# One core, float32 layers by split matmuls: the second weight product of the first layer as seven block products, with fourteen weight blocks rounded early into DRAM

## The chip, the cores and the metric

The kernel runs on one core of a Trainium2 chip. The time is device microseconds of one execution, taken as the median of three runs. Engines are named as in the profile: PE (matmuls), PEld (PE's weight loads), DVE, ACT and POOL (vector, scalar and general engines), SP (the queue that issues most DMAs).

## What is computed

A gated linear attention over `B, H, S, D = 2, 8, 768, 64`, then two feed-forward layers over its 1536 tokens of width 512:

```
state = gamma * state + k_t v_t^T ;  attn_t = scale * q_t state
x  = attn                       # (1536, 512)
h  = (x @ w_a) * (x @ w_b)      # (1536, 1536)
y  = h @ w_out                  # (1536, 512)
h2 = y @ w_in ; g = max(0.01 * h2, h2)     # (1536, 2048)
out = g @ w_out2                # (1536, 512)
```

The weights arrive as 64-bit floats, whose bits the kernel reads as pairs of 32-bit words and rounds to float32 itself.

## The kernel before

**Tiles.** All is held transposed: features on 128 partitions, tokens along the row, in three token tiles (t = 0, 1, 2) of 512. A weight block is 128 by 512. There are 12 blocks each of `a`, `b` and `wo` (the first layer, f = 0 to 11) and 16 each of `wi` and `wq` (the second, f = 0 to 15).

**Split matmuls.** A float32 operand is split in two (`split`, line 178): ACT casts it to the high part, DVE subtracts to get the low part. `mm3` (line 185) then issues three matmuls: high by high, high by low, low by high.

**Rounding a weight block.** SP loads 512 KB of raw bits into one of four buffers. `begin_weights` (line 213) has ACT take the magnitude (L220) and DVE the low word (L221); `round_steps` (line 225) adds four DVE instructions: sign (L235), scale and clip (L237), shift and or (L239), and the add of the low word (L243). Blocks are rounded in the order of the list `order`, and the raw buffer is loaded anew after it.

**First layer.** For each f, `ab_step` (line 444) runs 12 matmuls into bank `pa` (x by a) and 12 into `pb` (x by b) for one token tile; ACT copies `pa` out (L439), DVE multiplies the copy by `pb` (L441) and so makes h. `want` splits the next f's weights between the steps, and `ahead` rounds further blocks.

**y.** 36 steps of 12 matmuls follow (`y_mm`, line 463): each takes the split h of one token tile and one f, and adds to four banks over all f. Its side work is the split of h (L181, L182), of `wo`, and more rounding: 26 of the 32 blocks of the second layer are rounded before that layer begins.

**Second layer.** For each f (0 to 15, here called a block), three `h2_step`s make h2 for the three token tiles (12 matmuls each, one bank each; ACT scales it, L590, DVE takes the maximum, L591), and then one product of `Seven` is run. That class computes `g @ w_out2` as a 2 by 2 block product with 7 products in place of 8. The tokens are cut in two halves (tile 0 with half of tile 1, and half of tile 1 with tile 2), the inner index f in two halves, the columns of the weight in two. `prep` (line 113) makes the form of a product for one f: three ACT casts and three DVE subtractions (one of them 512 wide, two 256), and queues the sums of blocks that later products need; `product` (line 143) runs its matmuls: six of 512 columns and six of 256, into three banks. p1 and p7 run between the h2 steps, the other five by themselves after them. PSUM has eight banks; with p1 and p7 both open, two are left for the h2 steps. The last four `wi` blocks (f = 12 to 15) are rounded only when `want` asks for them, after the first h2 step of the block ahead (line 640).

## Time and profile before

| | us |
|---|---|
| median of 3 runs | 602.09 (602.02 to 602.2) |
| the profiled execution | 602.61 |
| its span, first to last instruction | 600.8 |
| PE busy in the span | 588.9 (98%) |
| DVE busy | 438.9 (73%) |
| ACT busy | 243.4 (41%) |
| POOL busy | 16.7 (3%) |

PE's busy time is modelled and overlaps from one matmul to the next, so the stages are measured from start to start: attention to 50.05 us, the first layer's `pa` and `pb` to 246.79, y to 344.71, then the second layer, whose last matmul starts at 596.69. The DMA queues move 52.26 MB at a mean of 87 GB/s.

### The profile page before, as it was taken

To read this page: it belongs to the slowest core of one execution; us is meant where nothing else is said; L and a number is where in the kernel's file an instruction comes from. 1 tells how busy PE (TensorE), PEld (TensorE's weight loads), DVE (VectorE), ACT (ScalarE), POOL (GpSimd) and SP (SyncE) were. 2 spreads that over 40 slices of the span, in tenths; PEclk is the share of its full clock that TensorE was granted. 3 is DMA by queue.
4 is the path that set the end of the run, shared out by engine and by line. 5 is a ranking of instruction groups with operands and counts; after the bars stand their busy time and mean duration, and the time that the engine had idled before them with its cause. 6 is when DMAs were issued, how large, how long until landed. Compare 5 with 4: busy or idle time off the path is not lost.

```text
span 600.8 us, 8357 instructions
## 1 busy us (share of the span) xinstructions
PE 588.9 (98%) x3175; PEld 492.1 (82%) x3175; DVE 438.9 (73%) x880; ACT 243.4 (41%) x499; POOL 16.7 (3%) x20
## 2 busy tenths in 40 slices
PE   6999999999999999999999999999999899999997
PEld 4888788888888888888888888888888777888886
DVE  3894667867777777996979575454666877969992
ACT  3763232223332324544343333333333336878710
POOL 3430000000000000000000000000000000000000
PEclk9999999999999999999999999999999999999999
DMA  8991223323423332321324220000000000010111
GB/s 300 385 355 37 71 105 141 124 91 136 141 105 117 130 123 91 138 78 64 141 78 166 72 71 0 1 0 1 1 1 0 2 0 2 1 53 2 53 53 53
DMA packets 19912, 52.26 MB, mean 87 GB/s; under 512 B 2336, under 2 KB 4000, under 8 KB 19872
## 3 DMA queue, kind: packets, MB, share of 16 engines
q1 hardware_dynamic: 19584, 51.45, 24.1%
q8 instruction: 25, 0.41, 0.3%
q10 hardware_dynamic: 288, 0.27, 0.2%
q14 instruction: 15, 0.12, 0.1%
HBM read 48.57 MB, written 3.15 MB: 86 GB/s over the span
## 4 chain that ended last, share of the span: by engine, by line
PE 94%; DVE 3%; ACT 1%; DMA 1%; issue 1%; POOL 0%; SPq 0%; DVEq 0%; POOLq 0%; ACTq 0%
PE h L187 7%; PE h L188 7%; PE h L189 7%; PE blk L188 6%; PE blk L187 6%; PE blk L189 6%; PE y L189 5%; PE y L187 5%; PE y L188 5%; PE pa L187 5%; PE pa L188 5%; PE pa L189 5%; PE pb L187 5%; PE pb L189 5%; PE pb L188 5%; PE sc L340 2%
## 5 line engine op out<-in xcount | busy, mean ns | idle before, releaser
L188 PE MATMUL blk<-form,form 128*128 128x512 f32 (+1 forms) x224 | 75.7, 338 | 0.0
L187 PE MATMUL blk<-form,form 128*128 128x512 f32 (+1 forms) x224 | 75.5, 337 | 0.0
L189 PE MATMUL blk<-form,form 128*128 128x512 f32 (+1 forms) x224 | 75.2, 336 | 0.0
L591 DVE TENSOR_TENSOR g<-g,h 128x512 f32<-128x512 f32 x48 | 32.6, 685 | 49.3 <-ACT g L590 49.3
L439 ACT COPY p<-pa 128x512 f32<-128x512 f32 x36 | 21.0, 587 | 106.9 <-PE pa L189 105.2
L590 ACT ACTIVATE g<-h 128x512 f32<-128x512 f32 x48 | 28.2, 596 | 86.4 <-PE h L189 86.4
L441 DVE TENSOR_TENSOR h<-p,pb 128x512 f32<-128x512 f32 x36 | 24.7, 686 | 47.6 <-PE pb L189 46.6
L125 ACT CAST form<-g 128x512 fp32r<-128x512 f32 x112 | 53.5, 513 | 12.0 <-DVE g L111 6.4
L126 DVE TENSOR_TENSOR form<-g,form 128x512 fp32r<-128x512 f32 x112 | 57.3, 553 | 0.9
L187 PEld LDWEIGHTS blk<-form,form 128*128 128x128 f32 x224 | 42.5, 190 | 5.4
L188 PEld LDWEIGHTS blk<-form,form 128*128 128x128 f32 x224 | 42.5, 190 | 5.0
L189 PEld LDWEIGHTS blk<-form,form 128*128 128x128 f32 x224 | 42.3, 189 | 4.7
L111 DVE TENSOR_TENSOR g<-g,g 128x512 f32<-128x512 f32 (+1 forms) x56 | 30.7, 573 | 0.3
L126 DVE TENSOR_TENSOR form<-wq,form 128x256 fp32r<-128x256 f32 x56 | 23.5, 420 | 9.2 <-ACT form L125 9.2
L125 ACT CAST form<-wq 128x256 fp32r<-128x256 f32 x56 | 22.7, 404 | 9.6 <-DVE wq L120 7.9
L346 DVE SCALAR_TENSOR_TENSOR P<-sc,small,causal 128x512 f32<-128x512 f32 x24 | 16.8, 742 | 7.4 <-PE sc L340 7.4
L322 POOL TENSOR_TENSOR qs<-q,cst 128x512 f32<-128x512 f32 x12 | 15.3, 1274 | 22.9 <-DMA q<-in_qT 21.4
L340 PE MATMUL sc<-qs,k 64*128 64x128 f32 x192 | 13.9, 285 | 1.5 <-POOL qs L322 1.5
L340 PEld LDWEIGHTS sc<-qs,k 64*128 64x128 f32 x192 | 11.6, 187 | 3.8 <-POOL qs L322 2.6
L319 ACT ACTIVATE kd<-n,small 128x256 f32<-128x256 f32 x24 | 10.9, 501 | 6.5 <-DMA n<-in_kn 6.4
L398 ACT COPY wk<-cr 64x192 f32<-64x192 f32 (+3 forms) x32 | 10.3, 323 | 6.1 <-DVE cr L381 5.5
L409 PE MATMUL xp<-P,v 128*64 128x128 f32 x192 | 12.6, 274 | 0.0
(3377 smaller groups left out, 1547.6 us busy)
## 6 DMA issues: line engine op xcount, KB each, us to landing
raw_wi<-in_w SPq DMA_DIRECT2D x16, 512.0 KB, 3.2
raw_wq<-in_w SPq DMA_DIRECT2D x16, 512.0 KB, 3.2
raw_a<-in_wab SPq DMA_DIRECT2D x12, 512.0 KB, 3.3
raw_b<-in_wab SPq DMA_DIRECT2D x12, 512.0 KB, 3.2
raw_wo<-in_wo SPq DMA_DIRECT2D x12, 512.0 KB, 3.2
q<-in_qT SPq DMA_DIRECT2D x12, 256.0 KB, 5.4
n<-in_kn SPq DMA_DIRECT2D x12, 256.0 KB, 5.3
v<-in_vn SPq DMA_DIRECT2D x12, 256.0 KB, 5.4
```

The lines of the kernel that those rows point to most:

```text
L111: queue.append(lambda piece=piece: run(*(self.A(*x[1:], j)[piece] for x in (d, x0, x1))))
L125: nc.scalar.copy(h, src)
L126: nc.vector.tensor_sub(l, src, h.bitcast(F32))
L187: nc.tensor.matmul(ps, w[0], x[0], start=first, stop=False, skip_group_check=more)
L188: nc.tensor.matmul(ps, w[0], x[1], start=False, stop=False, skip_group_check=more)
L189: nc.tensor.matmul(ps, w[1], x[0], start=False, stop=last, skip_group_check=more)
L340: nc.tensor.matmul(sc[h][:, c], d["k"][r, c], d["qs"][r, c], start=True, stop=True)
L346: nc.vector.scalar_tensor_tensor(pt.rearrange("p (j t) -> p j t", j=CPT), sc[h].rearrange("p (j t) -> p j t", j=CPT), small[:, n:n + 1], m ...
L439: nc.scalar.copy(a, pa)
L441: nc.vector.tensor_mul(h[t, f], a, pb)
L590: nc.scalar.mul(g[t, f], ps, 0.01)
L591: nc.vector.tensor_max(g[t, f], g[t, f], ps)
```

## The change

1. y is computed by the class `Seven` too, with `half` = 6: 42 products of 12 matmuls in place of 36 steps of 12. One of them runs after each f of the first layer (p1 for f = 1 to 6, p7 for f = 7 to 11), the others by themselves.
2. `Seven.prep` becomes a list of portions with a cost in us (`items`). In the first layer all side work (forms, sums, rounding, splits of weights) stands in a list `queue`, and `ab_step` issues 2.5 us of it after the copy of `pa` and 2.05 us after the multiplication by `pb`, 2.0 us more after each product.
3. `order` puts `wo` f-1 behind `a`, `b` f, and 14 blocks of the second layer (wi0 to wi6, wq0 to wq6) among those of the first (`PARK`). Each of the 14 is written to DRAM by a DMA on POOL's queue as soon as it is rounded, and SP loads it back at the end of y or the start of the second layer (`obtain`, `fetch`).
4. The second layer starts with token tile 2 for two values of f, and `want("wi", f + 1)` comes after the second h2 step of a block (after.py line 806) where it came after the first.

The diff, cut to its core:

```diff
 HALF = FF2 // 2
 QT = DM // 2
 LEAD = 3
+LEAD1 = 4
+PARK = (0, 1, 2, 2, 2, 1, 1, 1, 1, 1, 1, 1)
...
     def prep(self, n):
+        for _, run in self.items(n):
+            run()
+
+    def items(self, n):
...
+        def high():
+            hi, lo, x2, w2 = self.form_new(n)
+            (a5, a2), b2 = A(*a, j), B(*b, j)
+            for h, l, src in ((w2[:, 0:QT], w2[:, QT:], b2), (hi, lo, a5), (x2[:, 0:QT], x2[:, QT:], a2)):
+                nc.scalar.copy(h, src)
+                todo.append((l, src, h.bitcast(F32)))
+            todo.append(((hi, lo), (x2[:, 0:QT], x2[:, QT:]), w2))
+            low()
+
+        def low():
+            nc.vector.tensor_sub(*todo.pop(0))
+
+        def done():
+            low()
+            self.forms[n] = todo[0]
+            self.sums(name, j)
...
         if name == "p7":
-            nc.vector.tensor_sub(B(0, 1, j), B(1, 1, j), B(0, 1, j))
...
+            items.append((0.34, lambda: nc.vector.tensor_sub(B(0, 1, j), B(1, 1, j), B(0, 1, j))))
+        return items + [(0.34, high), (0.61, low), (0.34, done)]
...
+    park = ctx.enter_context(tc.tile_pool(name="park", bufs=1, space=bass.MemoryType.DRAM))
...
-    order = [(k, f) for f in range(FF1) for k in ("a", "b")]
-    order += [("wo", f) for f in range(FF1)]
...
     late_wi = [("wi", f) for f in range(FF2 - 4, FF2)]
-    order += [(k, f) for f in range(FF2) for k in ("wi", "wq") if (k, f) not in late_wi] + late_wi
+    second = [(k, f) for f in range(FF2) for k in ("wi", "wq") if (k, f) not in late_wi]
+    order, parked = [("a", 0), ("b", 0)], set()
+    for f in range(1, FF1 + 1):
+        order += [(k, f) for k in ("a", "b") if f < FF1] + [("wo", f - 1)]
+        for _ in range(PARK[f - 1]):
+            order.append(second.pop(0))
+            parked.add(order[-1])
+    first_layer = len(order)
+    order += second + late_wi
...
+        if key in parked:
+            dram[key] = park.tile([P, TT], F32, tag=f"{key[0]}{key[1]}", name=f"{key[0]}{key[1]}")
+            nc.gpsimd.dma_start(dram[key], rounded.pop(key))
+            slots.done(1)
...
+    queue = []
+
+    def pump(us):
+        while queue and us > 0:
+            cost, run = queue.pop(0)
+            run()
+            us -= cost
...
+    def until(done):
+        while queue and not done():
+            queue.pop(0)[1]()
...
+        def end():
+            next(steps[0], None)
+            at["queued"] -= 1
+            if at["queued"] and order[at["round"]] not in begun and at["round"] < at["load"]:
+                begin_weights()
+
...
+        at["queued"] += 1
+        queue.append((0.05, begin))
+        for cost in (0.34, 0.46, 0.72):
+            queue.append((cost, lambda: next(steps[0], None)))
+        queue.append((0.95, end))
+
...
+    def enqueue_split(key):
+        def high():
+            weights[key] = slots.new(F32R, f"{key[0]}{key[1]}h"), slots.new(F32R, f"{key[0]}{key[1]}l")
+            nc.scalar.copy(weights[key][0], rounded[key])
+
+        def low():
+            nc.vector.tensor_sub(weights[key][1], rounded.pop(key), as32(weights[key][0]))
+            slots.done(1)
+
+        queue.extend([(0.05, high), (0.61, low)])
...
+    def obtain(key):
+
+        until(lambda: key in rounded or key in dram)
+        while key not in rounded and key not in dram:
+            round_weights()
+        if key not in rounded:
+            rounded[key] = slots.new(F32, f"{key[0]}{key[1]}")
+            nc.sync.dma_start(rounded[key], dram.pop(key))
+
+    def fetch(n, reserve):
+        for key in list(dram)[:n]:
+            if slots.room() >= 1 + reserve:
+                obtain(key)
...
     def ab_step(t, f):
         pa, pb = bank(f"pa{t}{f}"), bank(f"pb{t}{f}")
         ab_mm(pa, t, f, 0, range(KC))
+        h[t, f] = slots.new(F32, f"h{t}{f}")
+        nc.scalar.copy(h[t, f], pa)
+        pump(2.5)
         ab_mm(pb, t, f, 1, range(KC))
-        ab_out(pa, pb, t, f)
+        nc.vector.tensor_mul(h[t, f], h[t, f], pb)
...
+        pump(2.05)
...
+    def y_split(i, o, m, src):
+
+        if m < 2:
+            y[2 * i, 2 * o + m] = split(src, f"y{i}{o}{m}")
+            return
+        for k in range(2):
+            key = (1, 2 * o + k)
+            if key not in y:
+                y[key] = slots.new(F32R, f"y{o}{k}h"), slots.new(F32R, f"y{o}{k}l")
+            hi, lo = (part[:, i * QT:(i + 1) * QT] for part in y[key])
+            piece = src[:, k * QT:(k + 1) * QT]
+            nc.scalar.copy(hi, piece)
+            nc.vector.tensor_sub(lo, piece, as32(hi))
+
...
+    def finish(z, u, leave):
+        for m in (2, 0, 1):
+            for n in range(len(z.plan) - 2, len(z.plan)):
+                z.product(n, [m])
+            leave(0, 1, [m], u["p1"], nc.vector.tensor_add, z.acc["p3"])
...
-    first = [(t, f) for f in range(1, FF1) for t in range(NTILE)]
-    for n, (t, f) in enumerate(first):
-        if t:
-            want("ab"[t - 1], f + 1)
-        if f == FF1 - 1:
-            h_split(0, t)
-            want("wo", t)
-        ab_step(t, f)
-        ahead(1.3)
...
-    for i, (t, f) in enumerate(late):
-        if i + 3 < len(late):
-            h_split(*late[i + 3])
-        if t == 0:
-            want("wo", f + 3)
-        if t == NTILE - 1 and f >= FF1 - 4:
-            if f >= FF1 - 2:
-                want("wi", f - FF1 + 2)
-        y_mm(t, f)
-        if f == FF1 - 1:
-            y_out(t)
-        slots.tick()
-        ahead(0.35 if t == 0 else 0.6, 9)
...
+    def form1_new(n):
+        new = tnew if n < FF1 - 1 else slots.new
+        return [make(F32R, f"forma{n}") for make in (new, new, tnew, tnew)]
...
+    z = Seven(nc, FF1 // 2, h, lambda f: once(wos, "wo", f), form1_new, blocks, mm3)
+    enqueue_round()
+    for f in range(1, FF1):
+        queue.extend(z.items(f - 1))
+        if f + 1 < FF1:
+            for k in "ab":
+                enqueue_round()
+                enqueue_split((k, f + 1))
+        enqueue_round()
+        for _ in range(PARK[f]):
+            enqueue_round()
+        for t in range(NTILE):
+            ab_step(t, f)
+            if t == 0 and f == FF1 - 1:
+                keep(z, u1, "p1")
+            if t == 1 and f == FF1 - 1:
+                for n in range(FF1 - 1, FF1 + LEAD1 - 2):
+                    queue.extend(z.items(n))
+        until(lambda: f - 1 in z.forms)
+        z.product(f - 1)
+        pump(2.0)
+        queue.extend(z.soon)
+        z.soon.clear()
+        slots.tick()
+    pump(1000)
+    for n in range(FF1 + LEAD1 - 2, FF1 + LEAD1 - 1):
+        z.prep(n)
...
+    H1 = FF1 // 2
+    for n in range(FF1 - 1, len(z.plan) - 2):
+        z.prep(n + LEAD1)
+        if n >= 3 * H1:
+            z.catch_up(2)
+        z.product(n)
+        slots.done(2)
+        slots.tick()
+        name, j = z.plan[n]
...
+        if n in (5 * H1, 6 * H1 - 2):
+            want("wi", int(n != 5 * H1))
+        if j == H1 - 1:
+            combine(z, u1, name, y_leave)
+        if n >= 5 * H1:
+            fetch(1, 12)
+        slots.tick()
+    finish(z, u1, y_leave)
+    slots.done(4 + 3 * H1 + 6)
+    slots.tick()
...
     for f in range(FF2):
-        h2_step(0, f)
-        slots.tick()
-        if f + 1 < FF2:
...
-        if f >= HALF:
-            z.prep(f)
...
-        for t in range(1, NTILE):
-            h2_step(t, f)
...
+        steps = [(t, f) for t in range(NTILE)]
+        if f < 2:
+            steps = [[(2, 0), (2, 1), (0, 0), (1, 0)], [(0, 1), (1, 1)]][f]
+        for n, step in enumerate(steps):
+            h2_step(*step)
             slots.tick()
+            if n == 0 and f == FF2 - 1:
+                keep(z, u2, "p1")
+            if n == 0 and f >= HALF:
+                z.prep(f)
+            if n == (f > 0):
+                if f + 1 < FF2:
+                    want("wi", f + 1)
+                else:
+                    z.prep(FF2)
         if f:
             z.product(f - 1)
         if f < HALF:
             z.prep(f)
         z.catch_up()
         slots.tick()
+        fetch(3, 6)
         if f < FF2 - 4:
-            ahead(1.4, 4)
+            ahead(1.5, 4, len(order) - len(late_wi))
```

What is left out: `combine`, `keep` and `leave` become functions of both layers, with the sums that they made before.

### How the instructions stand, before and now

DVE in the first layer, from one multiplication (L441, now L540) to the next. Names end in buffer numbers: `a8` is block f = 8 of w_a, `a8h`, `a8l` its high and low parts, `h17` is h of token tile 1 and f = 7, `pb17` its bank. Before, from tile 0 to tile 1 of f = 8:

```order
L441 TENSOR_TENSOR h08_237_1959<-p08_236_1957,pb08_1932 128x512
L235 TENSOR_SCALAR sign30_1961<-raw_wo6_1824 128x512
L237 TENSOR_SCALAR wo6_235_1927<-wo6_235_1927 128x512
L239 SCALAR_TENSOR_TENSOR wo6_235_1927<-wo6_235_1927,sign30_1961 128x512
L243 ISA wo6_235_1927<-wo6_235_1927,low30_1928 128x1024
L221 TENSOR_SCALAR low31_1969<-raw_wo7_1869 128x512
L182 TENSOR_TENSOR a9l_240_1973<-a9_193_1501,a9h_239_1972 128x512
L441 TENSOR_TENSOR h18_242_2004<-p18_241_2002,pb18_1977 128x512
```

Now, f = 7, up to the multiplication of tile 1; ahead of these twelve, behind the multiplication of tile 0, stand a subtraction of 256 columns and the low word of a8:

```order
L265 TENSOR_SCALAR sign32_2047<-raw_a8_1885 128x512
L267 TENSOR_SCALAR a8_207_2043<-a8_207_2043 128x512
L269 SCALAR_TENSOR_TENSOR a8_207_2043<-a8_207_2043,sign32_2047 128x512
L273 ISA a8_207_2043<-a8_207_2043,low32_2044 128x1024
L251 TENSOR_SCALAR low33_2055<-raw_b8_1916 128x512
L321 TENSOR_TENSOR a8l_211_2075<-a8_207_2043,a8h_210_2074 128x512
L265 TENSOR_SCALAR sign33_2078<-raw_b8_1916 128x512
L267 TENSOR_SCALAR b8_208_2054<-b8_208_2054 128x512
L269 SCALAR_TENSOR_TENSOR b8_208_2054<-b8_208_2054,sign33_2078 128x512
L273 ISA b8_208_2054<-b8_208_2054,low33_2055 128x1024
L251 TENSOR_SCALAR low34_2086<-raw_wo7_1960 128x512
L540 TENSOR_TENSOR h17_209_2072<-h17_209_2072,pb17_2059 128x512
```

Where four rounding steps, one low word and one split stood, there are now a whole rounding and most of the next one, and the parts of a form.

DVE where y's products begin to run by themselves (`forma14` is the form of product 14 of y, `h05` and `wo5` blocks that are summed). Before, at the first steps of y (`hs00l` is the low part of h):

```order
L182 TENSOR_TENSOR hs00l_2347<-h00_128_889,hs00h_2346 128x512
L182 TENSOR_TENSOR wo0l_278_2351<-wo0_211_1695,wo0h_277_2350 128x512
L441 TENSOR_TENSOR h011_280_2382<-p011_279_2380,pb011_2355 128x512
L235 TENSOR_SCALAR sign41_2384<-raw_wq2_2239 128x512
L237 TENSOR_SCALAR wq2_276_2342<-wq2_276_2342 128x512
L239 SCALAR_TENSOR_TENSOR wq2_276_2342<-wq2_276_2342,sign41_2384 128x512
L243 ISA wq2_276_2342<-wq2_276_2342,low41_2343 128x1024
```

Now, between the forms of products 13 and 14, the last eight of twelve sums and then the forms:

```order
L113 TENSOR_TENSOR h14_175_1560<-h14_175_1560,h110_241_2574 128x256
L113 TENSOR_TENSOR h05_184_1682<-h211_257_2795,h05_184_1682 128x512
L113 TENSOR_TENSOR h15_187_1739<-h111_255_2749,h15_187_1739 128x256
L110 TENSOR_TENSOR wo5_190_1752<-wo11_251_2722,wo5_190_1752 128x256
L113 TENSOR_TENSOR h25_193_1791<-h25_193_1791,h211_257_2795 128x512
L113 TENSOR_TENSOR h15_187_1739<-h15_187_1739,h111_255_2749 128x256
L110 TENSOR_TENSOR wo6_201_1918<-wo0_137_970,wo6_201_1918 128x256
L110 TENSOR_TENSOR wo7_212_2085<-wo1_143_1059,wo7_212_2085 128x256
L138 TENSOR_TENSOR forma14_2868<-wo8_223_2270,forma14_2868 128x256
L138 TENSOR_TENSOR forma14_265_2866<-h08_217_2184,forma14_264_2865 128x512
L138 TENSOR_TENSOR forma14_2867<-h18_219_2236,forma14_2867 128x256
L138 TENSOR_TENSOR forma15_2878<-wo9_234_2439,forma15_2878 128x256
```

The splits of h and of `wo` are gone; sums and forms of the block products stand in their place.

DVE in the second layer, block 12, around the rounding of wi13 (`g12`, `g112` are maxima of token tiles 0, 2 and 1, `form12` the form of product 12). Before, behind the maximum of tile 0:

```order
L221 TENSOR_SCALAR low65_4329<-raw_wi13_3305 128x512
L235 TENSOR_SCALAR sign65_4332<-raw_wi13_3305 128x512
L237 TENSOR_SCALAR wi13_416_4328<-wi13_416_4328 128x512
L239 SCALAR_TENSOR_TENSOR wi13_416_4328<-wi13_416_4328,sign65_4332 128x512
L243 ISA wi13_416_4328<-wi13_416_4328,low65_4329 128x1024
L182 TENSOR_TENSOR wi13l_418_4338<-wi13_416_4328,wi13h_417_4337 128x512
L120 TENSOR_TENSOR wq4_294_2524<-wq12_341_3241,wq4_294_2524 128x256
L126 TENSOR_TENSOR form12_4345<-wq4_294_2524,form12_4345 128x256
L126 TENSOR_TENSOR form12_4343<-g04_375_3685,form12_4342 128x512
L126 TENSOR_TENSOR form12_4344<-g14_378_3705,form12_4344 128x256
L591 TENSOR_TENSOR g112_4365<-g112_4365,h2112_4352 128x512
L591 TENSOR_TENSOR g12_4325<-g12_4325,h2212_4368 128x512
```

Now, behind the same maximum:

```order
L146 TENSOR_TENSOR wq4_362_3600<-wq12_417_4300,wq4_362_3600 128x256
L138 TENSOR_TENSOR form12_4773<-wq4_362_3600,form12_4773 128x256
L138 TENSOR_TENSOR form12_4771<-g04_399_4042,form12_4770 128x512
L138 TENSOR_TENSOR form12_4772<-g14_400_4058,form12_4772 128x256
L759 TENSOR_TENSOR g112_4793<-g112_4793,h2112_4780 128x512
L251 TENSOR_SCALAR low65_4797<-raw_wi13_4397 128x512
L265 TENSOR_SCALAR sign65_4800<-raw_wi13_4397 128x512
L267 TENSOR_SCALAR wi13_447_4796<-wi13_447_4796 128x512
L269 SCALAR_TENSOR_TENSOR wi13_447_4796<-wi13_447_4796,sign65_4800 128x512
L273 ISA wi13_447_4796<-wi13_447_4796,low65_4797 128x1024
L205 TENSOR_TENSOR wi13l_449_4806<-wi13_447_4796,wi13h_448_4805 128x512
L759 TENSOR_TENSOR g12_4766<-g12_4766,h2212_4809 128x512
```

The rounding and the split moved from ahead of the form and of the second maximum to behind both.

## Rows read from the trace of the kernel before

**Rows 1.** The page's head and its part 1, busy time of each engine
```profile
span 600.8 us, 8357 instructions
PE 588.9 (98%) x3175; PEld 492.1 (82%) x3175; DVE 438.9 (73%) x880; ACT 243.4 (41%) x499; POOL 16.7 (3%) x20
```

**Rows 2.** Busy time (and instructions) of each engine in three stretches, with the granted clock (PEclk)
```profile
core 0: us, PE busy (x) PEld busy (x) DVE busy (x) ACT busy (x) POOL busy (x), PEclk, DMA share, GB/s
246.80:344.70 97.90, 97.90 (x433) 81.07 (x432) 79.66 (x150) 40.70 (x71) 0.00 (x0) 1.00 0.30 103
344.70:508.80 164.10, 161.07 (x746) 134.18 (x745) 106.72 (x211) 59.20 (x122) 0.00 (x0) 1.00 0.02 7
508.80:600.80 92.00, 88.28 (x505) 77.19 (x503) 73.48 (x163) 51.22 (x124) 0.00 (x0) 1.00 0.10 35
```

**Rows 3.** Timeline of PE, first matmul of y and first of the second layer
```profile
246.79 0.39 PE L187 MATMUL y<-hs00h,wo0h 128*128 128x512 f32 x1
...
344.71 0.39 PE L187 MATMUL h<-y00h,wi0h 128*128 128x512 f32 x1
```

**Rows 4.** Timeline of PE, one block product in a stretch without waits
```profile
540.23 0.40 PE L187 MATMUL blk<-form,form 128*128 128x512 f32 x1
540.46 0.40 PE L188 MATMUL blk<-form,form 128*128 128x512 f32 x1
...
541.62 0.28 PE L187 MATMUL blk<-form,form 128*128 128x256 f32 x1
541.73 0.28 PE L188 MATMUL blk<-form,form 128*128 128x256 f32 x1
...
542.33 0.40 PE L187 MATMUL blk<-form,form 128*128 128x512 f32 x1
```

**Rows 5.** Timeline of PE, from the product ahead of block 12 into that block
```profile
465.58 0.28 PE L189 MATMUL blk<-form,form 128*128 128x256 f32 x1
466.61 0.50 PE L187 MATMUL h<-y00h,wi12h 128*128 128x512 f32 x1 [0.76 <-DVE g L591]
```

**Rows 6.** Timeline of DVE, what stands ahead of that PE wait
```profile
461.53 0.69 DVE L243 CUSTOM_DVE_ANT_0 wi<-wi,low 128x1024 uint16<-128x1024 uint16 x1
462.91 0.69 DVE L182 TENSOR_TENSOR wi12l<-wi,wi12h 128x512 fp32r<-128x512 f32 x1 [0.69 <-ACT wi12h L181]
...
464.93 1.03 DVE L126 TENSOR_TENSOR form<-g,form 128x512 fp32r<-128x512 f32 x2
465.88 1.28 DVE L591 TENSOR_TENSOR g<-g,h 128x512 f32<-128x512 f32 x2
```

**Rows 7.** Timeline of DVE, one rounding of a weight block and its split
```profile
72.97 0.69 DVE L441 TENSOR_TENSOR h<-p,pb 128x512 f32<-128x512 f32 x1 [2.12 <-PE pb L189]
73.58 0.42 DVE L221 TENSOR_SCALAR low<-raw_a 128x512 int32<-128x512 uint32 x1
...
74.25 0.42 DVE L237 TENSOR_SCALAR a<-a 128x512 f32<-128x512 f32 x1
74.70 0.69 DVE L239 SCALAR_TENSOR_TENSOR a<-a,sign 128x512 int32<-128x512 int32 x1
75.43 0.69 DVE L243 CUSTOM_DVE_ANT_0 a<-a,low 128x1024 uint16<-128x1024 uint16 x1
76.04 0.42 DVE L221 TENSOR_SCALAR low<-raw_b 128x512 int32<-128x512 uint32 x1
76.81 0.69 DVE L182 TENSOR_TENSOR a2l<-a,a2h 128x512 fp32r<-128x512 f32 x1 [0.35 <-ACT a2h L181]
```

**Rows 8.** A group of ACT by line and shape: xcount, busy us, mean ns, idle before
```profile
L439 ACT COPY p<-pa 128x512 f32<-128x512 f32 x36 | 21.0, 587 | 106.9 <-PE pa L189 105.2 <-PE pb L188 1.7
```

**Rows 9.** Timeline of POOL and of DVE in the attention stage, and POOL's line (min/median/max)
```profile
27.20 1.27 POOL L322 TENSOR_TENSOR qs<-q,cst 128x512 f32<-128x512 f32 x1 [1.47 <-DMA q<-in_qT]
...
27.61 1.15 DVE L235 TENSOR_SCALAR sign<-raw_a 128x512 int32<-128x512 int32 x1
...
L322 POOL TENSOR_TENSOR qs<-q,cst x12: 1264/1273/1286, 6.0 to 39.0; 128x512 f32<-128x512 f32 x12
```

168 lines of the change are left out of this document (77 added, 91 removed).

## The prediction

> **What bounds the kernel now.** I read the page's first part, the stages, and then the gaps between matmuls. PE is busy for 588.9 of 600.8 us [rows 1]. That figure is modelled, so I check it by starts. y runs from 246.79 to 344.71: 97.92 us for its 432 matmuls of 512 columns, 0.2267 us each [rows 3]. A block product in a quiet stretch takes 542.33 - 540.23 = 2.10 us [rows 4]: six matmuls of 512 columns at 0.23 and six of 256 at 0.12, no slower per column than y's. So each of these stretches is PE working without a pause, at a granted clock of 1.00 [rows 2], and only less PE work or fewer PE waits can shorten the kernel. DVE is the next busiest; it has 79.66 us of work in y's 97.90 [rows 2], so it has room, but not much.
>
> The waits that exist: between the last matmul of product 11 and block 12 of the second layer PE starts 1.03 us apart, where 0.12 is normal behind a matmul of 256 columns [rows 4, 5]. The releaser is DVE's maximum. Ahead of it DVE rounded wi12, stood idle 0.69 us for ACT's cast, split, made a form and came to the maxima at 465.88 [rows 6]. With p1 and p7 open there are two banks for h2, and the second is handed back by the second maximum. There are four such waits (blocks 12 to 15), 4 x 0.91 = 3.6 us.
>
> **DVE's prices**, from start to start: a two-input operation of 512 columns 0.61 (72.97 to 73.58), each fast step 0.335 (two from 73.58 to 74.25), then 0.45, 0.73 and 0.61 to the start of the next operation: one rounding is 2.46 us [rows 7]. A pair of 512 and 256 takes 0.95 (464.93 to 465.88), so 256 columns cost 0.34 [rows 6]. A split right behind its rounding, with one low word between, loses 0.35 waiting for ACT [rows 7].
>
> **The change, part by part.**
>
> *PE work.* y becomes 42 products of 2.10 us, 88.2 us against 97.92: **-9.7 us**. This is seven products for eight, so it cannot fail to be saved where PE is not made to wait.
>
> *First layer.* From f = 1 to 11, PE works 3 x 24 x 0.2267 + 2.10 = 18.4 us per f. DVE's heaviest are f = 2 to 4: five roundings 12.3, two splits 1.2, one form (0.34 + 0.61 + 0.34) 1.3, sums 1.3, three multiplications 1.8: 17.9, with the ACT wait 18.3. From f = 8 it is four roundings 9.8, splits 1.2, a p7 form 1.6, sums 2.2, multiplications 1.8: 16.7. So DVE fits, by 0.1 us at worst, with 1.7 in hand later. The order decides the rest: from f = 7 both accumulators are open and two banks remain, so `pb` of one step must be multiplied before `pb` of the next begins, 2.72 us later. The longest row is tile 0 to tile 1 at f = 7: behind the end of `pb` come 0.61 + 0.34 + 0.335, then the listed rows, 2.125 + 0.335 + 0.35 + 0.61 + 2.125 + 0.335, which puts the multiplication at 7.2 and its end at 7.9 us. PE wants the bank at 5.44 + 2.72 = 8.16. It holds with 0.2 us to spare. ACT has a copy of 0.59 [rows 8] in the same window, and one late cast eats the rest, so for the five blocks I take **+0.6** (bounds 0 and 5 x 0.91, the size of the waits that two banks make now [rows 5]).
>
> *Where the products run alone.* DVE comes to this stage without a lead. At f = 11, counted from the end of tile 0's `pb`: multiplication, form, a rounding and three steps of another end at 5.5; a multiplication, two steps and a sum at 7.8. The next forms wait for casts that stand behind ACT's copy of the third `pa` (8.16 + 0.59 = 8.75); nine subtractions and a multiplication end near 13.9, twelve sums (4 x 0.61 + 8 x 0.34) near 19.1. PE wants form 14 at 2 x 5.44 + 4 x 2.10 = 19.3, and its second subtraction ends only at 20.1: **+0.8** (bounds 0 and 2). From there to product 41 DVE has 28 forms, 36.1; 31 more operations of 512 columns, 18.9, and 18 of 256, 6.1; less the 3.7 behind the last product: 57.4. PE has 27 x 2.10 = 56.7. DVE is the slower by 0.7, and the last product wants its form's last part some 0.5 sooner than DVE gives it: **+1.2** (bounds 0, if ACT's and DVE's order leaves slack I do not see, and 5.6, below).
>
> *Stores and loads.* 14 roundings move from y to the first layer, counted above. The 14 stores run on POOL, which is idle from 50 us on, and the 14 loads on SP, whose queue holds nothing that is wanted before them. No row shows a store from POOL. The nearest is POOL's multiplication of 1.27 us, during which a DVE step that takes 0.42 elsewhere took 1.15 [rows 7, 9]. At 0.73 each the 14 would add 10 us to DVE, but each comes at an f's end, behind the last rounding, where the next multiplication is 7.5 us after the one before: taken as nothing. Against it, f = 2 to 4 hold two stores and 0.1 us of room; with five banks free there, a lag of some us costs PE nothing, and f = 5 and 6, with 15.4 us of DVE work, take it back.
>
> *Second layer.* The wait behind the maxima goes, as form and second maximum now stand ahead of the rounding: **-3.6**. Late next is the low part of wi. From the end of the first h2 step: maximum 1.3, form 3.7, second maximum 4.3, rounding 6.8, ACT's cast 7.4, low part 8.1; PE wants it at 2 x 2.72 + 2.10 + 0.45 = 8.0: +0.2 for each of four, **+0.8** (bounds 0 and 3.6, all as before). At its start, block 1 has two steps only, and wi2's low part stands behind a form, sums, a rounding and three maxima: about 8.6 us after the last step of block 0 where PE wants 8.0: **+0.5**. The 18 roundings left here are at most two to a block beside 10.26 us of PE work: no wait. The tail is unchanged.
>
> Sum: -9.7 - 3.6 + 0.6 + 0.8 + 1.2 + 0.8 + 0.5 = -9.4. The profiled execution took 602.61, 0.5 above the median, so 602.1 - 9.4 = **592.7 us**.
>
> **The rivals.**
>
> 1. *No new wait at all.* If ACT and DVE run somewhat closer than I add them, all five plus terms are nothing: 602.1 - 13.3 = 588.8. For it: DVE's work fits everywhere within 1 us. Against: at three places it fits with nothing left.
>
> 2. *DVE becomes the bound where products run alone.* Some sums read what the operation ahead wrote; the dependent scale step takes 0.45 where its neighbours take 0.335 [rows 7]. If each of 28 products costs DVE 0.2 us more than I count, PE waits 5.6 us more: 598.3. For it: 57.4 us of work against 56.7, no lead. Against: the second layer's own products ran alone with the same forms, and PE was busy for 88.28 of 92.00 us there, the tail of 3.9 us behind the last matmul among them [rows 2].
>
> 3. *The stores choke, and the kernel is slower.* In the first layer DVE has some 0.6 us in 18.4 free. POOL and DVE shut each other out in the one row that shows them together [rows 9]; there POOL came first. The Trainium skill says so as a rule (SBUF — State Buffer, "Who interferes with whom"): the port pair that the two share is held by one of them for a whole instruction, and a DMA from GpSimd's queue needs it for its descriptors. The trace agrees with the first half: 0.42 became 1.15 us; no run here shows the second. If 1.27 us of POOL work got only the gaps, a store would take two f, 39 us. Seven stores must be out by the last step of f = 7, when their buffers are reused, some 5.5 f or 101 us after the first; so it decides from 14 us a store. At 20 us each, PE waits 7 x 20 - 101 = 39 us: 632. Against: POOL's twelve multiplications kept 1.26 to 1.29 us beside a busy DVE [rows 9]. By the same skill (DMA: Bandwidth & Descriptors, "Anatomy of one DMA — SWDGE (gpsimd) path") a transfer of 262 KB is an estimated 2.0 + 0.6 = 2.6 us, far below 14.
>
> 4. *Two banks cost what they save.* If every step of f = 7 to 11 were late by 0.7 us, one DVE operation, 15 x 0.7 = 10.5 would go: 602.9, no change.
>
> **How the numbers follow.** The forecast, 590 to 596 us, gets 0.65; rival 1 0.13, rival 2 0.13, rival 3 0.05, rival 4 0.04. The range takes in the forecast, rival 1 and the lower half of rival 2: 588.6 to 597.5, which leaves out under 0.2. A measurement of this kernel can tell some 0.2%, 1.2 us, from no change. Faster by more than that: 0.65 + 0.13 + 0.13 = 0.91; the same 0.04; slower 0.05.
>
> **What would show it.** In the new profile, a y product should take PE 2.10 us wherever it runs; the gap into blocks 12 to 15 should fall from 1.03 to some 0.3 us, then released by the low part of wi. There should be a gap of about 0.8 us at product 14, released by DVE, and gaps of a few tenths after it. POOL's stores should land within 14 us. The forecast is wrong if the steps of f = 7 to 11 show a wait for the multiplication at each `pb`, if the product stage of y is longer than 31 x 2.10 + 3 us, or if anything waits for a store.

## The result and the profile after

| | before | after |
|---|---|---|
| median of 4 runs each, us | 602.06 (601.95 to 602.2) | **594.57** (594.24 to 595.14) |
| ratio | 1 | 0.9872, 95% interval 0.9859 to 0.9885 |
| span of the profiled execution | 600.8 | 593.2 |
| PE busy, share of the span | 588.9 (98%) | 583.0 (98%) |
| DVE busy, share of the span | 438.9 (73%) | 502.6 (85%) |

The kernel is 7.5 us faster; 592.7 was forecast, with 588.6 to 597.5 as the range. The head of the page and its part 1 answer to [rows 1]: PE does less, and DVE carries 64 us more, among it the forms and sums of 42 products.

```profile
span 593.2 us, 8767 instructions
PE 583.0 (98%) x3247; PEld 488.8 (82%) x3247; DVE 502.6 (85%) x1049; ACT 270.1 (46%) x587; POOL 24.6 (4%) x34
```

The first question is in which stage the 7.6 us of span went. The timeline of PE (start and length in us, line, tiles) gives the stage starts and the price of a product. Before, the first matmul of the first layer and the last of the second:

```profile
50.05 0.48 PE L187 MATMUL pa<-x0h,a0h 128*128 128x512 f32 x1
...
596.69 0.39 PE L189 MATMUL blk<-form,form 128*128 128x512 f32 x1
```

Now, the same two, with a product of y and the first matmul of the second layer between them:

```profile
50.31 0.48 PE L210 MATMUL pa<-x0h,a0h 128*128 128x512 f32 x1
...
280.04 0.40 PE L210 MATMUL blk<-forma,forma 128*128 128x512 f32 x1
...
282.14 0.40 PE L210 MATMUL blk<-forma,forma 128*128 128x512 f32 x1
...
337.51 0.39 PE L210 MATMUL h<-y100h,wi0h 128*128 128x512 f32 x1
...
589.16 0.39 PE L212 MATMUL blk<-form,form 128*128 128x512 f32 x1
```

A y product takes 282.14 - 280.04 = 2.10 us, as in [rows 4]. From the first `pa` to the first matmul of the second layer it was 344.71 - 50.05 = 294.66 us before [rows 3] and is 337.51 - 50.31 = 287.20 now: -7.46. From there to the last matmul it was 251.98 and is 251.65: only -0.33. Attention ends 0.26 us later, which says nothing: it ends anywhere from 49.18 to 51.10 in the runs below, whose code for it is the same. So the first layer and y gave what was forecast (-7.1), and the second layer, forecast at -2.3, gave almost nothing.

The busy time of each engine in three stretches (columns as in [rows 2]: PE, PEld, DVE, ACT and POOL with instructions in brackets, then the granted clock) shows where PE pauses. The first stretch ends where the product after f = 11 starts, the second is that product and the 31 after it, the third the second layer up to its own products alone:

```profile
50.31:268.18 217.87, 217.54 (x988) 180.53 (x986) 189.70 (x386) 78.96 (x151) 7.74 (x14) 1.00 0.39 136
268.18:337.51 69.33, 68.42 (x385) 59.02 (x384) 67.28 (x149) 43.27 (x108) 0.00 (x0) 1.00 0.17 54
337.51:501.23 163.72, 162.85 (x746) 133.71 (x745) 134.97 (x271) 67.12 (x135) 0.00 (x0) 1.00 0.13 46
```

PE waits for nothing between 84 and 268 us, from f = 2 to 11: two banks were enough. In the products alone DVE is busy 67.28 of 69.33 us. In the third stretch PE is idle 0.87 us by the model; the starts show more. Here is PE at the step into block 13, to be held against [rows 5]:

```profile
470.68 0.28 PE L212 MATMUL blk<-form,form 128*128 128x256 f32 x1
470.99 0.50 PE L210 MATMUL h<-y000h,wi13h 128*128 128x512 f32 x1
471.32 0.40 PE L211 MATMUL h<-y000l,wi13h 128*128 128x512 f32 x1
471.71 0.50 PE L212 MATMUL h<-y000h,wi13l 128*128 128x512 f32 x1
472.05 0.39 PE L210 MATMUL h<-y001h,wi13h 128*128 128x512 f32 x1
```

The single wait of 0.91 us is gone, and two have come in its place: 0.31 where 0.12 is normal (for wi13's high part), then 0.39 where 0.23 is normal (for its low part). Behind each of the two the next matmul also starts 0.33 to 0.34 us later in place of 0.23. Together 0.57 us, the same at blocks 14 and 15, and 0.51 at block 12: 2.2 us. What stands ahead of it, in the timeline of DVE and ACT (idle time before the instruction and its releaser in brackets):

```profile
465.68 0.42 DVE L138 TENSOR_TENSOR form<-wq,form 128x256 fp32r<-128x256 f32 x1 [0.48 <-ACT form L132]
...
467.14 0.68 DVE L759 TENSOR_TENSOR g<-g,h 128x512 f32<-128x512 f32 x1
467.74 0.42 DVE L251 TENSOR_SCALAR low<-raw_wi 128x512 int32<-128x512 uint32 x1
...
469.59 0.69 DVE L273 CUSTOM_DVE_ANT_0 wi<-wi,low 128x1024 uint16<-128x1024 uint16 x1
470.32 0.62 ACT L204 CAST wi13h<-wi 128x512 fp32r<-128x512 f32 x1 [2.79 <-DVE wi L273]
...
470.97 0.69 DVE L205 TENSOR_TENSOR wi13l<-wi,wi13h 128x512 fp32r<-128x512 f32 x1 [0.69 <-ACT wi13h L204]
```

The order is the one forecast. But DVE idles 0.48 us for the form's cast, and only then comes the second maximum and, behind it, the whole rounding.

Two further waits on a split, at block 2 and at block 9, on PE again:

```profile
356.14 0.40 PE L211 MATMUL h<-y000l,wi2h 128*128 128x512 f32 x1
357.10 0.50 PE L212 MATMUL h<-y000h,wi2l 128*128 128x512 f32 x1 [0.57 <-DVE wi2l L205]
...
428.91 0.40 PE L211 MATMUL h<-y000l,wi9h 128*128 128x512 f32 x1
429.52 0.50 PE L212 MATMUL h<-y000h,wi9l 128*128 128x512 f32 x1 [0.22 <-DVE wi9l L205]
```

At block 2 PE loses 0.85 us (0.96 for 0.23, then 0.34 for 0.23), at block 9 some 0.57. Last, the wait at product 14, where DVE, ACT and PE have to be read together:

```profile
265.66 0.59 ACT L537 COPY h<-pa 128x512 f32<-128x512 f32 x1 [4.23 <-PE pa L212]
...
266.58 0.43 DVE L138 TENSOR_TENSOR forma<-wo,forma 128x256 fp32r<-128x256 f32 x1 [1.29 <-ACT forma L132]
...
276.55 0.39 PE L210 MATMUL blk<-forma,forma 128*128 128x512 f32 x1
277.36 0.50 PE L211 MATMUL blk<-forma,forma 128*128 128x512 f32 x1 [0.41 <-DVE forma L138]
```

PE loses 0.58 + 0.11 us there, and some 1.5 us more at five shorter waits for forms up to 334 us. Ten us earlier DVE stood idle 1.29 us: the casts of product 11's form stand on ACT behind the copy of the third `pa`, and that waits for PE.

POOL's stores, by their line (seven of wi shown, the seven of wq likewise; duration ns, min/median/max, and first and last start; then the time to landing of all 14):

```profile
L279 POOL DMA_DIRECT2D wi<-wi x7: 539/542/712, 89.0 to 254.6; - x7
...
DMA to landing us min/median/max: 2.3/2.4/3.2
```

### The profile page after: what moved, and what is told of

The parts are those of the page before. It is cut to its first block, busy times and chain, and to the rows that moved or that the text cites. A ratio compares the mean times of both kernels' runs of the same rounds, so it can differ in the third digit from the quotient of the medians.

```text
span 593.2 us, 8767 instructions
## 1 busy us (share of the span) xinstructions
PE 583.0 (98%) x3247; PEld 488.8 (82%) x3247; DVE 502.6 (85%) x1049; ACT 270.1 (46%) x587; POOL 24.6 (4%) x34
## 4 chain that ended last, share of the span: by engine, by line
PE 79%; DVE 17%; ACT 2%; issue 1%; ACTq 0%; DVEq 0%
PE blk L211 8%; PE blk L210 8%; PE blk L212 8%; PE h L212 7%; PE h L210 7%; PE h L211 7%; DVE forma L138 6%; PE pa L210 5%; PE pa L211 5%; PE pa L212 5%; PE pb L212 5%; PE pb L210 5%; PE pb L211 5%; DVE h L113 2%; PE sc L431 1%
## 5 line engine op out<-in xcount | busy, mean ns | idle before, releaser
L537 ACT COPY h<-pa 128x512 f32<-128x512 f32 x33 | 19.4, 588 | 101.3 <-PE pa L212 101.3
L211 PE MATMUL blk<-forma,forma 128*128 128x512 f32 (+1 forms) x168 | 57.4, 342 | 0.9 <-DVE forma L138 0.7
L210 PE MATMUL blk<-forma,forma 128*128 128x512 f32 (+1 forms) x168 | 56.6, 337 | 0.0
L212 PE MATMUL blk<-forma,forma 128*128 128x512 f32 (+1 forms) x168 | 56.5, 336 | 0.0
L138 DVE TENSOR_TENSOR forma<-h,forma 128x512 fp32r<-128x512 f32 x84 | 42.9, 549 | 0.5
L132 ACT CAST forma<-h 128x512 fp32r<-128x512 f32 x84 | 38.8, 511 | 0.0
L211 PEld LDWEIGHTS blk<-forma,forma 128*128 128x128 f32 x168 | 31.8, 189 | 6.1 <-DVE forma L138 2.3
L210 PEld LDWEIGHTS blk<-forma,forma 128*128 128x128 f32 x168 | 31.8, 189 | 4.0
L212 PEld LDWEIGHTS blk<-forma,forma 128*128 128x128 f32 x168 | 31.7, 189 | 3.3
```

What stands on the lines that cost most here:

```text
L132: nc.scalar.copy(h, src)
L138: nc.vector.tensor_sub(*todo.pop(0))
L210: nc.tensor.matmul(ps, w[0], x[0], start=first, stop=False, skip_group_check=more)
L211: nc.tensor.matmul(ps, w[0], x[1], start=False, stop=False, skip_group_check=more)
L212: nc.tensor.matmul(ps, w[1], x[0], start=False, stop=last, skip_group_check=more)
L537: nc.scalar.copy(h[t, f], pa)
```

## The experiments

The theory after this reading: the second layer waits for the split of the next wi, by where the split stands, and y's waits come from the order of casts on ACT. The rivals: DVE's whole work is the bound; the stores on POOL slow DVE; two banks are too few. The table gives each run's median, its ratio to the kernel before with its interval, and two lengths from its profile: first layer and y (first `pa` to first h), and second layer (first h to last matmul).

| run | us | ratio | first layer and y | second layer |
|---|---|---|---|---|
| the changed kernel | 594.57 | 0.9872 (0.9859 to 0.9885) | 287.20 | 251.65 |
| e1_want_first | 596.47 | 0.9902 (0.9887 to 0.9916) | 287.20 | 252.83 |
| e2_want_mixed | 594.21 | 0.9865 (0.985 to 0.988) | 287.20 | 251.05 |
| e3_late_early | 592.6 | 0.9838 (0.9822 to 0.9855) | 287.25 | 249.37 |
| e4_park13 | 598.21 | 0.9937 (0.9919 to 0.9956) | 287.18 | 255.71 |
| e9_forms_first | 593.9 | 0.9858 (0.9843 to 0.9873) | 286.65 | 251.59 |
| e5_all | 590.93 | 0.981 (0.9795 to 0.9824) | 286.60 | 248.75 |
| e7_lumps | 601.75 | 0.9991 (0.9981 to 1.0) | 293.74 | 251.59 |
| e10_all_13 | 593.23 | 0.9847 (0.9823 to 0.9871) | 285.72 | 252.16 |
| e6_store_sp | 594.65 | 0.9869 (0.9855 to 0.9882) | 287.24 | 251.58 |
| e8_nopark | 626.49 | 1.0396 (1.0377 to 1.0415) | 297.80 | 272.41 |
| e11_moved_14 | **589.67** | **0.9788** (0.9775 to 0.9801) | 285.71 | 248.19 |
| e12_moved_15 | 589.64 | 0.9787 (0.9773 to 0.9801) | 285.75 | 247.89 |

### Where the split of the next wi stands

e1_want_first puts all splits behind the first h2 step:

```diff
-            if n == (f > 0):
+            if n == 0:
                 if f + 1 < FF2:
                     want("wi", f + 1)
```

> The changed kernel, with every split of the next wi put back behind the first h2 step of its block, late blocks included. Theory (the second layer still waits for the split of the next wi, and the place of the split decides which wait there is): the four late blocks get back the wait for the second maximum, 4 x 1.03 us in place of 4 x 0.57, +1.8; the wait at block 2 (0.85 us) mostly goes, -0.6, the one at block 9 (0.57 us) goes; together +0.7 us, about 595.3. Rival A (the place does nothing; what is late is DVE's whole work in that layer): within 0.3 us of the changed kernel. Rival B (the prediction's prices: the waits of 0.91 us come back and waits of 0.2 go): +2.8 us, 597.4.

Slower by 1.9 us in the median, 1.2 in the second layer's length. The late blocks lost what was expected: 1.03 us at each, from 458.87 on, and the wait at block 2 fell from 0.97 to 0.37 us between starts. What did not come is the gain at block 9: waits of 0.51 us in all turned up in block 10. So the place of the split matters at block 2 and at the late blocks, and not at block 9.

e2_want_mixed keeps the later place for the late blocks alone:

```diff
-            if n == (f > 0):
+            if n == (f >= FF2 - 5):
```

> The changed kernel, with the split of the next wi behind the first h2 step for blocks 2 to 11, and behind the second only for the four late blocks. Theory (the waits at blocks 2 and 9 come from the split standing behind a maximum that it need not stand behind): both go or shrink to 0.3 us, -1.1 us, 593.5, with the late blocks as they were. Rival A (DVE's whole work is late there, after two roundings in a row): the waits turn up at another instruction, within 0.3 us of the changed kernel.

The second layer is 0.60 us shorter, all of it at block 2; the median's -0.36 is within the runs' spread. Block 9's wait moved to block 10's start (0.37 us where 0.12 is normal). The theory holds for block 2 and the rival for block 9: there DVE had two roundings in a row behind it (both done at 424.85 in the changed kernel, just ahead of block 8's form), and is late wherever the split stands.

### The late roundings in two parts

e3_late_early fills DVE's idle time ahead of the form with the rounding's first steps:

```diff
-            if n == 0 and f >= HALF:
+            if n == 0 and FF2 - 5 <= f < FF2 - 1:
+                part = round_steps()
+                items = [run for _, run in z.items(f)]
+                for run in items[:-3] + [lambda: next(part)] * 2 + items[-3:]:
+                    run()
+            elif n == 0 and f >= HALF:
                 z.prep(f)
...
+                if FF2 - 5 <= f < FF2 - 1:
+                    for _ in part:
+                        pass
                 if f + 1 < FF2:
                     want("wi", f + 1)
```

> The changed kernel, with the roundings of the four late wi in two parts: magnitude, low word, sign and scale ahead of the form of p7, shift and add behind the second maximum as before. Theory (the low part of wi ends 0.45 us too late at blocks 12 to 15, and DVE stands idle 0.48 us ahead of the form for ACT's cast): the low part comes 0.55 us earlier, the four waits of 0.57 us go, -2.2 us, 592.4. Rival (DVE's work per block, not its order, is the bound; the form and the second maximum come 0.45 us later and a wait turns up there): between -0.5 and 0.

As the theory said: -2.0 us in the median, -2.28 in the second layer. The timeline of DVE shows three steps of the rounding in the time for which it used to wait, and the split's low part starts at 469.17, 0.71 us ahead of block 13's first matmul:

```profile
464.20 0.42 DVE L251 TENSOR_SCALAR low<-raw_wi 128x512 int32<-128x512 uint32 x1
464.53 0.42 DVE L265 TENSOR_SCALAR sign<-raw_wi 128x512 int32<-128x512 int32 x1
464.87 0.42 DVE L267 TENSOR_SCALAR wi<-wi 128x512 f32<-128x512 f32 x1
465.21 0.42 DVE L138 TENSOR_TENSOR form<-wq,form 128x256 fp32r<-128x256 f32 x1
...
469.17 0.69 DVE L205 TENSOR_TENSOR wi13l<-wi,wi13h 128x512 fp32r<-128x512 f32 x1 [0.69 <-ACT wi13h L204]
```

And PE goes into block 13 without a pause:

```profile
469.76 0.28 PE L212 MATMUL blk<-form,form 128*128 128x256 f32 x1
469.88 0.40 PE L210 MATMUL h<-y000h,wi13h 128*128 128x512 f32 x1
```

### Where y's waits come from

e4_park13 leaves one rounding, at f = 11, to the second layer:

```diff
-PARK = (0, 1, 2, 2, 2, 1, 1, 1, 1, 1, 1, 1)
+PARK = (0, 1, 2, 2, 2, 1, 1, 1, 1, 1, 1, 0)
```

> The changed kernel, with 13 weight blocks rounded into DRAM in place of 14: the rounding of wq6 at the end of the first layer (2.46 us of DVE) is left to the second layer. Theory (DVE's work bounds the products that run alone in y, without a lead): the waits at product 14 and behind it, 2.2 us in all, go, and the second layer takes the rounding beside its 10.26 us of PE per block: -2.0 us, 592.6. Rival A (those waits come from the order of casts and forms): they stay, within 0.4 us of the changed kernel. Rival B (the work is only handed on, and the second layer waits for it): the stage of y is shorter by 2 us and the second layer longer by as much.

The theory missed: 2.46 us less DVE work ahead of y's products, and the stage is as long as before (287.18). DVE only idles longer for the same casts, 2.55 us in place of 1.29:

```profile
267.35 0.42 DVE L138 TENSOR_TENSOR forma<-wo,forma 128x256 fp32r<-128x256 f32 x1 [2.55 <-ACT forma L132]
```

So rival A holds for these casts, and rival B's second half too: the second layer is 4.06 us longer. There DVE rounds two blocks in a row at 442.70 to 447.28 with two banks left, and PE waits for the first maximum of block 10:

```profile
445.45 0.39 PE L212 MATMUL h<-y11h,wi10l 128*128 128x512 f32 x1
448.01 0.50 PE L210 MATMUL h<-y100h,wi10h 128*128 128x512 f32 x1 [2.18 <-DVE g L759]
...
449.65 0.63 PE L210 MATMUL h<-y110h,wi10h 128*128 128x512 f32 x1
450.08 0.63 PE L211 MATMUL h<-y110l,wi10h 128*128 128x512 f32 x1
```

The wait costs 2.3 us, and from 449.65 on matmuls start 0.43 us apart for some three us, at a lower granted clock: 1.6 us more (see the last section). Of the four runs two show that clock in their mean (0.997: 598.47 and 600.14, the profiled one) and two do not (1.000: 597.74 and 597.96), so the median stands between the two.

e9_forms_first issues two forms ahead of the last step of the first layer:

```diff
                 for n in range(FF1 - 1, FF1 + LEAD1 - 2):
                     queue.extend(z.items(n))
+                until(lambda: FF1 in z.forms)
```

> The changed kernel, with the forms of products 11 and 12 issued ahead of the last step of the first layer, so that their casts on ACT stand ahead of the copy of the third pa and no longer behind it. Theory (the waits at product 14 and behind it come from ACT's order: DVE stands idle 1.29 us for these casts at 266.58 and never makes it up): DVE has that much lead, the wait of 0.69 us at product 14 goes and those behind it shrink, -1.2 us, 593.4. Rival A (DVE's work in the stage bounds it, whatever its lead): the later waits grow by what is saved, within 0.3 us of the changed kernel. Rival B (the copy of the third pa is wanted sooner, and the multiplication and PE wait for it): slower by 0.3 to 1 us.

Half of it: -0.7 us in the median, -0.55 in the stage. DVE's idle time for the cast falls to 0.47 us, and the wait at product 14 is gone; the waits behind it stay. That DVE's work is what counts for those is shown by e10_all_13 below: with the forms first and one rounding less, the stage is another 0.9 us shorter.

```profile
265.48 0.43 DVE L138 TENSOR_TENSOR forma<-wo,forma 128x256 fp32r<-128x256 f32 x1 [0.47 <-ACT forma L132]
```

e5_all has the edits of e2_want_mixed, e3_late_early and e9_forms_first together:

> Three edits at once on the changed kernel: the mixed place of the split, the late roundings in two parts, and the forms of products 11 and 12 ahead of the last step of the first layer. Theory (three separate waits): the gains add, -0.4, -2.0 and -1.2 us, 591.0. Rival (what one edit frees is taken by the next wait): 592.0 to 592.6, no better than the late roundings in two parts alone.

The three edits together give -3.6 us, against -0.4, -2.0 and -0.7 alone. In the lengths they add to within 0.05 us: -0.60 in the first layer and y against -0.55 alone, -2.90 in the second layer against -0.60 and -2.28. So these are separate waits, and what one edit frees is not taken by another.

### Portions, stores and DRAM

e7_lumps issues the first layer's side work once a step:

```diff
-        pump(2.5)
+        pass
...
-        pump(2.05)
+        pump(4.55)
```

> The changed kernel, with the first layer's side work issued in one portion of 4.55 us behind each multiplication by pb in place of two of 2.5 and 2.05. Theory (DVE has the work done in time either way; pb's bank is wanted 2.1 us after the multiplication could run, and a portion of 4.55 fits between two of them): 0 to +1.5 us, 595.3. Rival A (the portions are what keeps PE going with two banks): a wait of 0.7 us or more at each step of f = 7 to 11, +10 us or more. Rival B (fewer interleavings save ACT's waits): -0.5 us.

Slower by 7.2 us, nearly all of the change's gain, so rival A is nearer in size; but its place is another. PE waits for the copy of `pa`, not for the multiplication (waits of PE in 84 to 345 us: total, times, longest):

```profile
PE blk L211 <- DVE forma L138: 2.9, 3, 2.3
PE pa L210 <- ACT h L537: 2.5, 4, 1.7
```

The lump's work on ACT stands ahead of the copy: at f = 8 ACT is at the magnitude of `a` until the copy's start at 207.02, and PE starts the next `pa` 0.66 us behind the last `pb` in place of 0.23. At f = 9 and 10 it is the same, at f = 11 it is 2.11 us, as ACT's three copies of p1's banks (L576) stand there too: 3.6 us in all. Most of the rest is lost at product 14, to which DVE comes later still: 2.73 us between starts there in place of 0.81. In two portions the copy stands between them. (The profiled run, 601.37, and one other, 600.70, have a mean granted clock of 1.000; the other eight, 601.3 to 602.6, have 0.997.)

e6_store_sp moves the stores to SP's queue:

```diff
-            nc.gpsimd.dma_start(dram[key], rounded.pop(key))
+            nc.sync.dma_start(dram[key], rounded.pop(key))
```

> The changed kernel, with its 14 stores to DRAM issued on SP's queue in place of POOL's. Theory (the stores cost nothing on POOL: no DVE instruction beside one is stretched): within 0.3 us, 594.6. Rival A (POOL's issuing shuts DVE out for a part of each store): -0.5 to -2 us. Rival B (a store on SP holds up the weight loads behind it): +1 us or more.

No change (594.65 against 594.57, ratio 0.9869 against 0.9872). The stores cost nothing that the time shows on POOL's queue, and on SP's neither.

e8_nopark rounds nothing early:

```diff
-PARK = (0, 1, 2, 2, 2, 1, 1, 1, 1, 1, 1, 1)
+PARK = (0,) * 12
...
-            ahead(1.5, 4, len(order) - len(late_wi))
+            ahead(2.0, 4, len(order) - len(late_wi))
```

> The changed kernel without the early roundings: no block goes through DRAM, and the second layer rounds 28 blocks, up to two after each block. Theory (DVE has 17 us idle from the second layer's start to block 11, and 14 more roundings are 14 x 2.46 = 34 us): PE waits some 17 to 25 us there, the waits in y go (-1.9), 610 to 618, slower than the kernel before. Rival (the second layer has room for the roundings): 593 to 597.

Slower than the kernel before by 24 us and than the changed kernel by 32. The second layer grew by 20.8 us, as expected; that y's waits would go was wrong: y grew by 10.6, since the splits of wi0 and wi1 now bring their roundings into it. Not all of this is waiting: behind some of the pauses the granted clock is 0.50, for 17.1 us in four stretches (from 336.6, 343.4, 370.7 and 486.8), where matmuls start 0.43 us apart. By these starts that is some 6 of the 32 us. The largest wait of PE in the second layer up to 503 us:

```profile
PE h L210 <- ACT wi12h L204: 8.0, 1, 8.0
```

So the change depends on the early roundings through DRAM: without them DVE has no room, at the end of y and in the second layer, for both the roundings and the block products.

### A better version

e10_all_13 is e5_all with 13 blocks and another rate of rounding in the second layer:

```diff
-PARK = (0, 1, 2, 2, 2, 1, 1, 1, 1, 1, 1, 1)
+PARK = (0, 1, 2, 2, 2, 1, 1, 1, 1, 1, 1, 0)
...
-            ahead(1.5, 4, len(order) - len(late_wi))
+            ahead(2.0 if f < 7 else 1.0, 4, len(order) - len(late_wi))
```

> The three edits at once, with 13 blocks rounded into DRAM in place of 14, and the second layer's rounding ahead at two a block up to block 6 and one a block from 7. Theory (the 2.57 us wait of the 13-block run came from two roundings in a row in a late block; early blocks have room for two): y's waits go by another 0.6 us and nothing is given back, 590.4. Rival A (two roundings in every early block are over DVE's room): waits at blocks 1 to 7, slower than the three edits alone by 1 to 3 us.

Half of it came true: y's stage is 0.9 us shorter than with the three edits. But rival A came true as well, slower than the three edits by 2.3 us in the median, though with one wait and not with many: at block 2, after two roundings behind block 0.

```profile
354.60 0.40 PE L211 MATMUL h<-y000l,wi2h 128*128 128x512 f32 x1
357.44 0.80 PE L212 MATMUL h<-y000h,wi2l 128*128 128x512 f32 x1 [2.44 <-DVE wi2l L205]
```

That one place costs 4.25 us by the starts from 354.60 on, some 1.5 of it by a lower granted clock. The four runs differ in that: 591.65 and 592.17 at a mean clock of 1.000, 594.29 (profiled) and 594.52 at 0.997. Hence e11_moved_14, on top of the three:

```diff
-PARK = (0, 1, 2, 2, 2, 1, 1, 1, 1, 1, 1, 1)
+PARK = (0, 1, 2, 2, 2, 2, 1, 1, 1, 1, 1, 0)
...
-            ahead(1.5, 4, len(order) - len(late_wi))
+            ahead(2.0 if 0 < f < 7 else 1.0, 4, len(order) - len(late_wi))
```

> The three edits, the rounding at f = 11 moved to f = 5 (two blocks rounded into DRAM there, none at 11), and the second layer's rounding ahead at one block after block 0, two after blocks 1 to 6, one after 7 to 11. Theory (a rounding costs nothing where DVE has room for it, and it has 3 us at f = 5): y's stage is as in the 13-block run, -0.9 us, and the waits at blocks 10 and 11 go, -0.5: 589.5. Rival (f = 5 has no room, or two roundings after each early block are too many): waits there, 591 to 593.

589.67, as expected, and faster than both kernels: y's stage is 0.89 us shorter than with the three edits alone, the second layer 0.56. In that layer, up to 500 us, PE is now busy throughout by the model (by the starts 0.26 us are left, at block 2):

```profile
336.90:500.00 163.10, 163.10 (x762) 136.34 (x761) 137.13 (x279) 70.34 (x143) 0.00 (x0) 1.00 0.14 46
```

e12_moved_15 goes one further:

```diff
-PARK = (0, 1, 2, 2, 2, 2, 1, 1, 1, 1, 1, 0)
+PARK = (0, 1, 2, 2, 2, 2, 2, 1, 1, 1, 1, 0)
...
-            ahead(2.0 if 0 < f < 7 else 1.0, 4, len(order) - len(late_wi))
+            ahead(0.0 if f == 0 else 2.0 if f < 7 else 1.0, 4, len(order) - len(late_wi))
```

> As the run with 14 moved, with a fifteenth block rounded into DRAM at f = 6 and none rounded after block 0. Theory: the wait of 0.36 us at block 2 goes too, 589.1. Rival (f = 6 leaves DVE behind when two banks remain from f = 7 on): waits at f = 7, 590 to 592.

The second layer is 0.30 us shorter still and f = 7 shows no wait, but the median is the same (589.64): the difference is below what the runs tell.

## Why the prediction was right, and where its sum was off

**PE work, -9.7.** Right: 2.10 us a product, wherever it runs alone.

**First layer, +0.6 for two banks.** PE pauses for nothing between 84 and 268 us, so the lower bound, nothing, was the value. It was closer than the 0.2 us that the prediction found: at f = 7 the multiplication of tile 1 runs from 191.06 to 191.74, and PE starts the `pb` that wants its bank at 191.78, without a pause. And the margin is there only with the portions: with lumps it is the copy of `pa`, which the prediction had as an ACT operation "in the same window", that comes too late.

**Products alone, +0.8 and +1.2.** Measured 0.69 at product 14 and some 1.5 behind it. The working came out step by step: counted from the end of tile 0's `pb` at f = 11 (257.30), the sums end at 19.0 us (forecast 19.1), form 14 is wanted at 19.25 (19.3) and its second subtraction ends at 19.9 (20.1). The step that named the cause was right for product 14, "the next forms wait for casts that stand behind ACT's copy of the third `pa`": the run with the forms first took that wait away, and e4_park13, with less DVE work and the same casts, did not. For the waits behind it the prediction named DVE's work (57.4 us against PE's 56.7). That is right too, for some 0.9 of the 1.5 us, which went when the work did, in e10_all_13. The other 0.66 us, at 332 to 334 where the last two products begin, stay in every later run; they answer to the forecast's "some 0.5 sooner" for the last product. The 31 products take 67.3 us, below the 31 x 2.10 + 3 = 68.1 at which the forecast would have been wrong.

**Stores and loads, nothing.** Right: the same time with the stores on SP, and no 14 us anywhere, the longest landing being 3.2 us; of DVE's instructions beside the 14 stores three were stretched, from 0.42 us to between 0.47 and 0.49, 0.17 us in all. By the Trainium skill (DMA: Bandwidth & Descriptors, "Anatomy of one DMA — SWDGE (gpsimd) path") a store of this size takes an estimated 2.6 us; the median of 2.4 agrees. The rule of the Trainium skill on the shared port pair (SBUF — State Buffer, "Who interferes with whom"), by which a DMA from GpSimd's queue needs that pair for its descriptors, may be what stretched these three; no run here shows the port itself. Rival 3 falls. (Its row, [rows 9], shows DVE held up beside POOL, and not POOL beside DVE.)

**Second layer, -3.6 + 0.8 + 0.5 = -2.3.** This is the step that failed; measured -0.33. (a) The old waits are gone as said; with the slower matmul behind each they were worth 4 x 1.03 = 4.1 us. (b) "+0.2 for each of four" was 0.51 to 0.57, so 2.2 in place of 0.8. From the end of the first h2 step the low part was put at 8.1 us against a want at 8.0; in block 12 the next step starts at 463.29, and the low part ends 8.3 us later, at 471.58. Besides these 0.2 us the sum had two things missing: the high part is late as well, so that the step into the block shows 0.31 us as forecast but for another cause, and each wait slows the matmul behind it by 0.11. (c) "+0.5" at block 2 was 0.85. (d) "At most two to a block beside 10.26 us of PE work: no wait" was wrong at block 9, 0.57 us: with p7's form and sums in the block there is no room for two roundings in a row. -4.1 + 2.2 + 0.85 + 0.57 is -0.5, against the -0.33 of the profile. That these places are the cause is shown by the runs that cleared them: the late roundings in two parts gave back 2.28 us, the mixed place 0.60, and e11_moved_14, with one rounding behind each of blocks 7 to 11, the rest but 0.26.

So the total came out inside the range because the terms of the first layer and y, which carry most of it, were right to 0.4 us (-7.46 against -7.1); the 2.0 us that the second layer did not give were taken up by the width of the range and not by the sum.

**Rivals 1, 2 and 4** fall: the waits were not nothing, the products alone lost 2.2 us and not 5.6 more than forecast, and the steps of f = 7 to 11 were not late. (Rival 4's time should read 602.6 by its own numbers, 592.7 - 0.6 + 10.5.)

## What to carry to other kernels

When a wait is removed by moving work behind it, the work that was moved has its own due time: work out when its last instruction ends, and do not trust a margin of one or two tenths either way. Here a forecast margin of 0.2 us held, by 0.04, and a lateness forecast at 0.1 or 0.2 us cost over half a microsecond. Where an engine is idle ahead of a form, see whether it waits for a cast that stands behind an evacuation in another engine's order, as here; move the cast, or put an independent step into the gap. Saving PE work with more DVE work pays only if that DVE work finds room in another stage: here the products were worth 9.7 us, and without the roundings moved early the kernel was 32 us slower.
